# Two PV steps behind fourteen rounds in the MLP's groups of four slots

## The chip, the cores and the metric

The kernel runs on one core of one Trainium2 chip. The metric is the device time of one execution in microseconds, the median of several runs. Its engines are TensorE (PE, with its weight loads shown apart as PEld), VectorE (DVE), ScalarE (ACT), GpSimd (POOL) and SyncE (SP), whose queue issues nearly all DMAs.

## The reference

The program computes `x + s * g` in fp32, for 2048 tokens of width 512. `s` is multi-head attention of the layer-normalised input with 32 heads of width 16, and `g` the SiLU of a two-layer MLP with a squared ReLU.

```python
def _A_ref(x, wqkv, wo):
    B, S, D = x.shape                       # 1, 2048, 512
    H = 32
    Dh = D // H
    qkv = (lambda x, *d: x.transpose(*d))((x @ wqkv).reshape(B, S, 3, H, Dh), 2, 0, 3, 1, 4)
    q, k, v = qkv[0], qkv[1], qkv[2]
    scores = jnp.einsum("bhqd,bhkd->bhqk", q, k) * (Dh ** -0.5)
    p = _softmax(scores, axis=-1)
    o = jnp.einsum("bhqk,bhkd->bhqd", p, v)
    return (lambda x, *d: x.transpose(*d))(o, 0, 2, 1, 3).reshape(B, S, D) @ wo

def _B_ref(x, w1, b1, w2, b2):
    h = jnp.einsum("bsd,df->bsf", x, w1) + b1      # df: 512 x 1792
    zero = jnp.zeros_like(h)
    r = jnp.where(h > zero, h, zero)
    h = r * r
    out = jnp.einsum("bsf,fd->bsd", h, w2) + b2
    return out

x = A_x
xn = _layernorm(x, axis=-1)
s = _A_ref(xn, A_wqkv, A_wo)
g = _silu(_B_ref(xn, B_w1, B_b1, B_w2, B_b2))
return x + s * g
```

## The kernel before

**Two passes over the scores.** The softmax needs the maximum of each row of scores. The kernel computes the scores twice. The first time (`max_mm`, L298 and L305) a matmul puts 128 x 512 scores into a PSUM bank and VectorE reduces them to 128 maxima. The second time (`exp_mm`, matmul at L1234, exp at L1246) a matmul with the maxima folded in as extra rows puts 512 queries against 128 keys into another bank, and ScalarE takes the exp into an SBUF tile. A PV step (`pv_step`, `pv_mm`, L373) then multiplies the exps of four heads with their values into one accumulating bank `po`.

**Units and slots.** A unit is four heads by 512 queries; there are 32. A unit has 16 slots, one for each block of 128 keys, so there are 512 slots. One slot has four maxima (of slot + 24, `LEAD`), four exps and one PV step (of slot - 2).

**Row tiles.** Scores and dense matmuls contract over 64 rows at most, so TensorE is used as two tiles of 64 rows, "lanes" 0 and 1, that run side by side. A round is one operation on each lane. PV contracts over 128 rows with 32 columns a head: four matmuls side by side, and two passes of them to a step, fp32. In the profile the shapes `64*128` and `128*32` tell the two arrangements apart.

**The dense work.** While attention runs, the generator `dense` hands out the MLP and the output projection in pieces. Each matmul of the reference there is three matmuls, of high and low parts (`terms3`). `first_pair` makes two 256-wide halves of the hidden layer in the bank `pd_t`, `second` makes 128 tokens of the output. Both yield groups of work by `block`: 12 units on lane 0 and 12 on lane 1, for four slots. In `first_pair` a unit is two matmuls of 256 columns, in `second` one of 512. The other forms of slot (`slot`, `plain_slot`) do not change here.

**The groups of four slots.** `long_slots` writes out the order of four slots as two halves, `for h in range(2)`. In half `h` the 12 dense units (`D`) stand on lane `h`; beside them are maxima (`m`) and exps (`s`) of the other lane. Before the change a half has two parts: ten rounds of a maximum or an exp beside a unit, then what ends a slot, with its PV step; then four rounds (two units, each beside a maximum; two exps; an exp and a maximum), and the end of the second slot with its PV step. `post`, behind the last unit of a dense bank, lets ScalarE take that bank away: two Relus (L526) for `first_pair`, a copy (L547) for `second`. `last_use` is the ScalarE instruction after which the other lane may write the dense bank.

**What ends and begins a slot.** `max_end` (loads of K and Q for later units, and at a unit's end VectorE's last maximum, L325), `shift_due` (VectorE turns the maxima into the rows that the exps' matmuls use, L335 to L338; they go through DRAM) and `begin`, which sets the clock `now` and runs what `later` has put off until that slot: DMAs, the reciprocal of the sums (`evac_recip`, L397), the tanh of the gate (`gate`, L553) and others.

**Order and buffers.** The program's order on every engine is that in which the code emits (`manual_schedule`), and each engine's queue runs in order. A matmul that waits for a bank holds all that stands behind it. PSUM's eight banks are split between the pools `pe` (3, exps' scores), `pm` (3, maxima's scores), `pd` (1, dense) and `pv` (1, PV):

```python
pe = ph.enter_context(tc.tile_pool(name="pe", bufs=3, space=PSUM))
pm = ph.enter_context(tc.tile_pool(name="pm", bufs=3, space=PSUM))
pd = ph.enter_context(tc.tile_pool(name="pd", bufs=1, space=PSUM))
pv = ph.enter_context(tc.tile_pool(name="pv", bufs=1, space=PSUM))
```

A pool gives its banks out in turn. The tiles of exps in SBUF are a ring of 17 (`NPT`), of which `exp_mm` takes the oldest that no open slot holds.

Of the kernel before, what the change touches and what calls it, by code (L numbers as in the profile page):

```python
# [19 lines left out]
D = 512  # L20
# [8 lines left out]
LEAD = 24  # L29
# [5 lines left out]
EVAC = (1, 6, 7, 9, 11, 14)  # L35
EVAC_LAST = (1, 3, 4, 5, 7, 9)
GAPS = (18, 19, 20, 22)
EPS = 1e-5


@with_exitstack
def kernel(
# [31 lines left out]
    eps_t = const.tile([P, 1], F32, name="eps_t")  # L74
    nc.vector.memset(eps_t, EPS)
    b1_t = const.tile([P, FO], F32, name="b1_t")
# [22 lines left out]
    with ExitStack() as ph:  # L99
# [42 lines left out]
        def load_k(qd, n):  # L142

            p, j, i = n // 6, n // 3 % 2, n % 3
            if n % 6 == 0:
                kas[qd, p] = ring("ka")
            h = 4 * qd + 2 * p + j
            nc.sync.dma_start(
                kas[qd, p][64 * j + DH * i : 64 * j + DH * (i + 1), :].bitcast(F32),
                k_d[h // 8][i % 2, (h % 8) * DH : (h % 8 + 1) * DH, :],  # L150
            )
# [20 lines left out]
        def load_q_pair(u, name, p, tiles):  # L172
                qd, qc = divmod(u, 4)
                t = ring(name)
                for j in range(2):
                    load_head(
                        t, j, q_d, 4 * qd + 2 * p + j, (0, 0, 1), slice(qc * 512, (qc + 1) * 512)
                    )
                tiles.append(t)

        late = []
        last_use = [None]
# [9 lines left out]
        def run_waiting(all_=False):  # L192
            due = [w for w in waiting if all_ or w[0] <= now[0]]
            waiting[:] = [w for w in waiting if w not in due]
            for _, fn in due:
                fn()
# [92 lines left out]
        def max_mm(g, j, bank=None):  # L289
            u = g // 16  # L290
            qd = u // 4
            if u not in mxs:
                mxs[u] = sp.tile([P, 16, 4], F32, name="mx")
                for i in range(2):
                    togo[u, i] = [(p, qb, kc) for p in range(2) for qb in range(4) for kc in range(4)]
            p, qb, kc = togo[u, j].pop(0)
            ps = pm.tile([P, 512], F32, name="pm_t") if bank is None else bank()
            nc.tensor.matmul(  # L298
                ps,
                qms[u][p][64 * j : 64 * j + 64, qb * P : (qb + 1) * P],  # L300
                kas[qd, p][64 * j : 64 * j + 64, kc * 512 : (kc + 1) * 512],
                start=True, stop=True,
            )
            c = (2 * p + j) * 4 + qb
            return nc.vector.tensor_reduce(  # L305
                mxs[u][:, c, kc : kc + 1], ps, axis=AX.X, op=ALU.max
            )

        def max_end(g):
            u, s = divmod(g, 16)  # L310
            if u >= NU:
                return
            qd, qc = divmod(u, 4)
            if qc == 2 and qd + 1 < NQ and s % 2 == 0:
                load_k(qd + 1, s // 2)
            if qc == 3 and qd + 1 < NQ and s % 2 == 0 and s < 8:
                load_k(qd + 1, 8 + s // 2)
            if s in (7, 8):
                load_q_pair(u, "qe", s - 7, qes.setdefault(u, []))
            if s in (9, 11) and u + 1 < NU:  # L320
                load_q_pair(u + 1, "qm", (s - 9) // 2, qms.setdefault(u + 1, []))
            if s == 15:
                assert not togo[u, 0] and not togo[u, 1]
                m4 = m4s[u % 2]
                nc.vector.tensor_reduce(m4[:, :16], mxs[u], axis=AX.X, op=ALU.max)  # L325
                mxs[u] = m4
                late.append((g + 2, u))

        def shift_due(g):
            if late and late[0][0] <= g:  # L330
                shift(late.pop(0)[1])

        def shift(u):
            tr = sp.tile([P, 32], F32, name="tr", bufs=1)
            nc.vector.transpose(tr, mxs[u])  # L335
            sh = sp.tile([P, 2, 32], F32R, name="sh", bufs=1)
            nc.vector.tensor_scalar(sh[:, 0], tr, -1.0, None, op0=ALU.mult)
            nc.vector.scalar_tensor_tensor(  # L338
                sh[:, 1], tr, -1.0, sh[:, 0].bitcast(F32),
                op0=ALU.mult, op1=ALU.subtract,  # L340
            )

            def keep():
                nc.sync.dma_start(
                    sh_d[u].rearrange("b c i n -> (b c) i n"), sh.bitcast(F32)
                )

            def back():
                for p in range(2):
                    for i in range(2):  # L350
                        shift_rows(u, p, i)

            if in_loop:
                later(1, keep)
                later(2, back)
            else:
                keep()
                back()
# [242 lines left out]
        def right(stk, name, bufs):  # L601
            return stk.enter_context(tc.tile_pool(name=name, bufs=bufs, side="right"))
# [75 lines left out]
        def wo_ask(k):  # L678

            c, tt = divmod(k % 16, 4)  # L680
            t0 = c * 512 + tt * P
            g = wos["f"].tile([P, D], F32, name="g", bufs=6)
            nc.sync.dma_start(g, g_d[t0 : t0 + P, :])
            if k < 16:
                t = wos["oc3"].tile([P, D], F32, name="xr", bufs=3)
                nc.sync.dma_start(t, xf[t0 : t0 + P, :])
            elif c < 2:
                t = wos["f"].tile([P, D], F32, name="s")
                nc.sync.dma_start(t, sp_d[t0 : t0 + P, :])
            else:  # L690
                t = tail[c, tt]
            wos[k] = g, t
# [30 lines left out]
        def wo_last(c):  # L723
            for tt in range(4):
                k = 16 + 4 * c + tt
                wo_ask(k + 2)
                if k in GAPS:
                    yield None, None
# [160 lines left out]
        st = right(ln, "wq_st", 1)  # L889
# [296 lines left out]
        for rnd in range(2 * LEAD):  # L1186
# [32 lines left out]
            if g % 2 and g < 16:  # L1219
                c, i = divmod(g // 2, 2)  # L1220
# [29 lines left out]
        def pv_step(st, pts):  # L1250
            u, kb = divmod(st, 16)
            if kb == 0:
                pos[0] = pv.tile([P, 512], F32, name="po")
            pv_mm(pos[0], u // 4, kb, pts)
            if kb == NT - 1:
                if u < NU - 2:
                    evac(pos[0], u)
                elif u == NU - 2:
                    unit_inner(pos[0])
                else:  # L1260
                    unit_final(pos[0])
# [21 lines left out]
        pts = {}  # L1283
# [58 lines left out]
        def long_slots(st0, units, post):  # L1342


            g0 = st0 + LEAD
            todo = [[(st0 + k, j) for k in range(4) for j in (lane, lane + 2)] for lane in range(2)]
            for kb in range(st0, st0 + 4):
                pts.setdefault(kb, {})

            def s(lane):  # L1350
                kb, j = todo[lane].pop(0)
                return exp_mm(kb, j, pts[kb], False)

            for h in range(2):
                own, other = units[h], 1 - h
                for part, (mine, theirs) in enumerate((("D" * 10, "msmsmsmsms"), ("DDss", "mmsm"))):
                    st = st0 + 2 * h + part
                    if st > st0:
                        begin(st)
                    for i, ops in enumerate(zip(mine, theirs)):  # L1360
                        for lane in (h, other) if part else (other, h):
                            o = ops[0] if lane == h else ops[1]
                            if o == "D":
                                own.pop(0)()
                            elif o == "m":
                                max_mm(g0, lane)
                            else:
                                use = s(lane)
                                if part and lane == h and i == 2:
                                    last_use[0] = use  # L1370
                        if part and h and i == 1 and post is not None:
                            post()
                    max_end(st + LEAD)
                    shift_due(st + 1 + LEAD)
                    pv_step(st - 2, pts.pop(st - 2))
            if post is not None:
                last_use[0] = None
            assert not todo[0] and not todo[1] and not units[0] and not units[1]
# [17 lines left out]
        def begin(st):  # L1396
            now[0] = st
            if st % 64 == 48 and st // 64 + 1 < NQ:
                load_v(st // 64 + 1)
            run_waiting()  # L1400
# [63 lines left out]
```

## Time and profile before

| | |
|---|---|
| time, median of 3 runs | 1638.31 us (1637.2 to 1639.26) |
| span of the profiled execution | 1635.6 us |
| granted TensorE clock | 0.999 |
| TensorE matmul busy | 1620.8 us, 99% |
| weight loads busy | 923.2 us, 56% |
| VectorE busy | 1356.8 us, 83% |
| ScalarE busy | 1189.9 us, 73% |
| GpSimd busy | 523.0 us, 32% |

For the profiled execution the span is given, from its first instruction to its last; the time around it isn't shown apart, and the median of the runs is 2.7 us above that span. Busy time of TensorE counts every stretch in which some matmul runs. Matmuls are pipelined, so the start of one to the start of the next is often shorter than a row's duration, and it is the distance between starts that tells the pace. In a timeline, rows of one kind that follow each other are merged, with their count at the end and the time from the first start to the last end.

### The profile page before, as it was taken

To read this page: it belongs to the slowest core of one execution; us is meant where nothing else is said; L and a number is where in the kernel's file an instruction comes from. 1 tells how busy PE (TensorE), PEld (TensorE's weight loads), DVE (VectorE), ACT (ScalarE), POOL (GpSimd) and SP (SyncE) were. 2 spreads that over 40 slices of the span, in tenths; PEclk is the share of its full clock that TensorE was granted. 3 is DMA by queue.
4 is the path that set the end of the run, shared out by engine and by line. 5 is a ranking of instruction groups with operands and counts; after the bars stand their busy time and mean duration, and the time that the engine had idled before them with its cause. 6 is when DMAs were issued, how large, how long until landed. Compare 5 with 4: busy or idle time off the path is not lost.

```text
span 1635.6 us, 35352 instructions
## 1 busy us (share of the span) xinstructions
PE 1620.8 (99%) x13300; PEld 923.2 (56%) x13300; DVE 1356.8 (83%) x2345; ACT 1189.9 (73%) x2351; POOL 523.0 (32%) x547
## 2 busy tenths in 40 slices
PE   8999999999999999999999999999999999999998
PEld 6777565456546655664466456645654565445543
DVE  6356888888888888888888888888888888887754
ACT  7311777777777777877777777777777777777786
POOL 6446568123112311321133112311321233125421
PEclk9999999999999999999999999999999999999999
DMA  8768655434333333434343334323532353246654
GB/s 299 193 210 276 205 171 145 125 100 124 83 95 100 109 93 81 129 87 112 79 121 89 83 90 141 101 68 88 147 98 61 88 144 81 60 130 195 193 170 155
DMA packets 164418, 209.18 MB, mean 128 GB/s; under 512 B 59928, under 2 KB 78872, under 8 KB 162712
## 3 DMA queue, kind: packets, MB, share of 16 engines
q1 hardware_dynamic: 163960, 206.40, 44.5%
q8 instruction: 105, 1.72, 0.5%
q14 instruction: 65, 0.53, 0.1%
q10 hardware_dynamic: 288, 0.52, 0.1%
HBM read 149.95 MB, written 56.61 MB: 126 GB/s over the span
## 4 chain that ended last, share of the span: by engine, by line
PE 99%; DVE 1%; DMA 0%; issue 0%; ACT 0%; POOL 0%; DVEq 0%; POOLq 0%
PE po L373 31%; PE pd_t L242 18%; PE pm_t L298 18%; PE se L1234 15%; PE pd_t L210 6%; PE pd_t L972 2%; PE po L972 2%; PE se L1019 1%; PE se L972 1%; PE pd_t L1019 1%; PE se L298 1%; PE po L1019 1%; PE pm_t L1234 1%; PE pm_t L1065 0%; PE pm_t L811 0%; DVE mx L305 0%
## 5 line engine op out<-in xcount | busy, mean ns | idle before, releaser
L305 DVE TENSOR_REDUCE mx<-pm_t 128x1 f32<-128x512 f32 x2000 | 1245.1, 684 | 167.8 <-PE pm_t L298 77.3
L1246 ACT ACTIVATE pt<-se 128x512 f32<-128x512 f32 x2002 | 1044.2, 617 | 257.6 <-PE se L1234 214.5
L298 PE MATMUL pm_t<-ka,qm 64*128 64x512 f32 x2000 | 793.7, 420 | 1.5 <-DVE mx L305 1.3
L1234 PE MATMUL se<-qe,ka 64*128 64x512 f32 x2002 | 674.0, 396 | 0.2 <-ACT pt L1246 0.2
L373 PE MATMUL po<-pt,v 128*32 128x512 f32 x4096 | 545.3, 604 | 0.0
L298 PEld LDWEIGHTS pm_t<-ka,qm 64*128 64x128 f32 x2000 | 350.1, 184 | 244.8 <-DVE mx L305 230.7
L242 PEld LDWEIGHTS pd_t<-xc,w1s 64*128 64x128 f32 x2688 | 334.0, 187 | 93.9 <-issue 88.9
L242 PE MATMUL pd_t<-xc,w1s 64*128 64x256 f32 x2688 | 380.2, 288 | 0.0
L1234 PEld LDWEIGHTS se<-qe,ka 64*128 64x128 f32 x2002 | 337.6, 184 | 20.7 <-ACT pt L1246 2.6
L242 PE MATMUL pd_t<-w2t,hT 64*128 64x512 f32 x1080 | 300.6, 410 | 0.0
L242 PEld LDWEIGHTS pd_t<-w2t,hT 64*128 64x128 f32 x1080 | 179.1, 184 | 80.5 <-issue 75.5
L529 POOL TENSOR_TENSOR r<-r 128x512 f32<-128x512 f32 x56 | 58.2, 1040 | 374.9 <-ACT r L526 374.9
L373 PEld LDWEIGHTS po<-pt,v 128*32 128x32 f32 x4096 | 81.0, 108 | 158.8 <-issue 136.4
L548 POOL TENSOR_TENSOR u<-u,b_t 128x512 f32<-128x512 f32 x16 | 20.6, 1287 | 316.3 <-ACT u L547 316.3
L411 POOL TENSOR_TENSOR ot<-ot,hl 128x512 f32<-128x512 f32 x31 | 39.8, 1284 | 204.4 <-DMA hl<-r_d 91.1
L210 PE MATMUL pd_t<-wot,oc 64*128 64x512 f32 x336 | 90.9, 406 | 0.0
L526 ACT ACTIVATE r<-pd_t,b_t 128x256 f32<-128x256 f32 x112 | 46.9, 470 | 57.1 <-PE pd_t L242 57.1
L210 PEld LDWEIGHTS pd_t<-wot,oc 64*128 64x128 f32 x336 | 58.4, 184 | 45.4 <-ACT pt L1246 14.2
L84 POOL TENSOR_TENSOR hT<-r,hT 128x512 fp32r<-128x512 f32 x56 | 72.2, 1290 | 4.7
L210 PE MATMUL pd_t<-w2t,hT 64*128 64x512 f32 x264 | 68.8, 393 | 0.0
L305 DVE TENSOR_REDUCE mx<-se 128x1 f32<-128x512 f32 x48 | 32.9, 685 | 40.0 <-PE pm_t L298 30.0
L210 PEld LDWEIGHTS pd_t<-w2t,hT 64*128 64x128 f32 x264 | 47.0, 184 | 6.0
(129 smaller groups left out, 928.5 us busy)
## 6 DMA issues: line engine op xcount, KB each, us to landing
w1s<-w_d SPq DMA_DIRECT2D x196, 256.0 KB
qm<-q_d SPq DMA_DIRECT2D x384, 32.0 KB
ka<-k_d SPq DMA_DIRECT2D x96, 128.0 KB
qe<-q_d SPq DMA_DIRECT2D x384, 32.0 KB
xn_d<-xT SPq DMA_DIRECT2D x8, 1024.0 KB
k_d<-hl SPq DMA_DIRECT2D x32, 256.0 KB
q_d<-hl SPq DMA_DIRECT2D x32, 256.0 KB
xc<-xn_d SPq DMA_DIRECT2D x16, 512.0 KB
```

The lines of the kernel that those rows point to most:

```text
L84: (lo or nc.gpsimd).tensor_tensor(dst[1], raw, dst[0].bitcast(F32), op=ALU.subtract)
L210: mm = nc.tensor.matmul(out_, lh(r), rh(r), start=first_ and lane == 0, stop=last_ and lane == 1, skip_group_check=True,)
L242: mm = nc.tensor.matmul(out_, lh(r), rh(r), start=first_ and lane == 0, stop=last_ and lane == 1, skip_group_check=True,)
L298: nc.tensor.matmul(ps, qms[u][p][64 * j : 64 * j + 64, qb * P : (qb + 1) * P], kas[qd, p][64 * j : 64 * j + 64, kc * 512 : (kc + 1) * 512] ...
L305: return nc.vector.tensor_reduce(mxs[u][:, c, kc : kc + 1], ps, axis=AX.X, op=ALU.max)
L373: nc.tensor.matmul(po[32 * j : 32 * j + 32, :], vs[qd][:, (4 * kb + j) * VW : (4 * kb + j) * VW + 32], pts[j], start=(kb == 0), stop=(kb = ...
L526: nc.scalar.activation(r[:, i], ps[:, i * CW : (i + 1) * CW], AF.Relu, bias=b1_t[:, fo : fo + 1])
L529: nc.gpsimd.tensor_tensor(r, r, r, op=ALU.mult)
L972: nc.tensor.matmul(out_[:, n0:n1], lh(slice(0, P)), rh(slice(0, P))[:, n0:n1], start=first_, stop=last_,)
L1019: nc.tensor.matmul(out_, lh(slice(0, P)), rh(slice(0, P)), start=first_, stop=last_)
L1234: nc.tensor.matmul(se, kas[qd, j // 2][b : b + 64, kb * P : (kb + 1) * P], qes[u][j // 2][b : b + 64, :], start=True, stop=True,)
L1246: return nc.scalar.activation(pts[j], se, AF.Exp, scale=0.25)
```

## The change

In `long_slots` the two parts of a half become one. The order of what stands beside the 12 dense units is written out in `BESIDE`: six maxima and six exps of the other lane. Round 13 is an exp on each lane, round 14 a maximum on each. Then come, for both slots, `max_end` and `shift_due`, and then both PV steps. `begin` of the second slot runs ahead of the eighth round. In each half the dense operation is now written behind the other lane's in every round; `last_use` is the exp of the own lane, the last exp of the half; and `post` follows it. Over a half the counts stay: 12 units, 8 maxima, 8 exps, 2 PV steps. The other lane now has seven maxima and seven exps in a half and the own lane one each, where they had eight and none, and six and two.

```diff
+BESIDE = "msmssmmssmsm"
...
             for h in range(2):
                 own, other = units[h], 1 - h
-                for part, (mine, theirs) in enumerate((("D" * 10, "msmsmsmsms"), ("DDss", "mmsm"))):
-                    st = st0 + 2 * h + part
-                    if st > st0:
-                        begin(st)
-                    for i, ops in enumerate(zip(mine, theirs)):
-                        for lane in (h, other) if part else (other, h):
-                            o = ops[0] if lane == h else ops[1]
-                            if o == "D":
-                                own.pop(0)()
-                            elif o == "m":
-                                max_mm(g0, lane)
-                            else:
-                                use = s(lane)
-                                if part and lane == h and i == 2:
-                                    last_use[0] = use
-                        if part and h and i == 1 and post is not None:
-                            post()
-                    max_end(st + LEAD)
-                    shift_due(st + 1 + LEAD)
-                    pv_step(st - 2, pts.pop(st - 2))
+                st = st0 + 2 * h
+                if h:
+                    begin(st)
+                for i, o in enumerate(BESIDE):
+                    if i == 7:
+                        begin(st + 1)
+                    if o == "m":
+                        max_mm(g0, other)
+                    else:
+                        s(other)
+                    own.pop(0)()
+                s(other)
+                last_use[0] = s(h)
+                if h and post is not None:
+                    post()
+                for lane in (other, h):
+                    max_mm(g0, lane)
+                for k in (st, st + 1):
+                    max_end(k + LEAD)
+                    shift_due(k + 1 + LEAD)
+                for k in (st, st + 1):
+                    pv_step(k - 2, pts.pop(k - 2))
             if post is not None:
                 last_use[0] = None
```

## The prediction

> **What bounds the kernel now.** I read the page's busy times, its chain and its costliest groups first.
>
> ```profile
> span 1635.6 us, 35352 instructions
> PE 1620.8 (99%) x13300; PEld 923.2 (56%) x13300; DVE 1356.8 (83%) x2345; ACT 1189.9 (73%) x2351; POOL 523.0 (32%) x547
> PE 99%; DVE 1%; DMA 0%; issue 0%; ACT 0%; POOL 0%; DVEq 0%; POOLq 0%
> L305 DVE TENSOR_REDUCE mx<-pm_t 128x1 f32<-128x512 f32 x2000 | 1245.1, 684 | 167.8 <-PE pm_t L298 77.3
> L1246 ACT ACTIVATE pt<-se 128x512 f32<-128x512 f32 x2002 | 1044.2, 617 | 257.6 <-PE se L1234 214.5
> ```
>
> TensorE ends everything: the chain is 99% PE. But VectorE is 83% busy, nearly all of it maxima. So PE can be relieved by only a little before the maxima matter.
>
> Next the timeline of TensorE over one half of a group (a half is two slots, one pass of `for h`). Columns: start, duration, engine, line, names, count.
>
> ```profile
> 703.40 0.50 PE L298 MATMUL pm_t<-ka,qm 64*128 64x512 f32 x1
> 703.74 0.39 PE L1234 MATMUL se<-qe,ka 64*128 64x512 f32 x1
> 703.98 0.39 PE L298 MATMUL pm_t<-ka,qm 64*128 64x512 f32 x1
> ...
> 705.62 0.39 PE L1234 MATMUL se<-qe,ka 64*128 64x512 f32 x1
> 705.98 1.07 PE L373 MATMUL po<-pt,v 128*32 128x512 f32 x8
> 706.98 0.49 PE L298 MATMUL pm_t<-ka,qm 64*128 64x512 f32 x1
> ...
> 707.78 0.39 PE L298 MATMUL pm_t<-ka,qm 64*128 64x512 f32 x1
> 708.10 1.07 PE L373 MATMUL po<-pt,v 128*32 128x512 f32 x8
> 709.10 0.49 PE L298 MATMUL pm_t<-ka,qm 64*128 64x512 f32 x1
> ```
>
> Ten rounds, a PV step, four rounds, a PV step, with no hole in it: PE itself is the bound. A round takes 0.235 us (703.74 to 705.62 is eight of them). The first round after a PV step takes 0.34 (703.40 to 703.74), a PV step 1.00 until the next round, and from the last round to the PV step it is 0.32 (707.78 to 708.10) and not 0.235.
>
> How long the halves are, from the same view: 14 halves of first-layer groups (two 256-wide matmuls to a unit) lie between the first two rows, 6 of the second layer (one 512-wide) between the others.
>
> ```profile
> 657.80 0.49 PE L298 MATMUL pm_t<-ka,qm 64*128 64x512 f32 x1
> 737.61 0.50 PE L298 MATMUL pm_t<-ka,qm 64*128 64x512 f32 x1
> 783.30 0.49 PE L298 MATMUL pm_t<-ka,qm 64*128 64x512 f32 x1
> 817.27 0.49 PE L298 MATMUL pm_t<-ka,qm 64*128 64x512 f32 x1
> ```
>
> That is 5.70 and 5.66 us a half. By the loops there are 56 first-layer and 45 second-layer groups, so 112 and 90 halves, 202 in all.
>
> **The change, part by part.**
>
> *Removed: a switch in and out of the PV steps, per half.* The trace has two PV steps behind each other once, at the very end (PE rows, then weight loads of the same stretch):
>
> ```profile
> 1620.07 3.03 PE L373 MATMUL po<-pt,v 128*32 128x512 f32 x24
> ```
>
> ```profile
> 1620.07 0.16 PEld L373 LDWEIGHTS po<-pt,v 128*32 128x32 f32 x8 [0.36 <-issue]
> 1620.53 0.13 PEld L373 LDWEIGHTS po<-pt,v 128*32 128x32 f32 x4 [0.30 <-issue]
> 1620.96 0.13 PEld L373 LDWEIGHTS po<-pt,v 128*32 128x32 f32 x4 [0.30 <-issue]
> 1621.39 0.81 PEld L373 LDWEIGHTS po<-pt,v 128*32 128x32 f32 x8 [0.30 <-ACT pt L1246]
> ```
>
> A step is two sets of four matmuls, and the sets start 0.43 us apart. So a second step adds 0.86, and a pair takes 1.00 + 0.86 = 1.86 until the next round. If nothing waits, the new half is 0.34 + 12 x 0.235 + 0.32 + 1.86 = 5.34 us: 0.36 less, or 0.32 in the second layer. Over 112 and 90 halves that is a gain of about 69 us. The counts of matmuls, maxima and exps are unchanged (per half 8 maxima, 8 exps, 12 units, 2 PV steps).
>
> *Added: waits for score banks.* The maxima's banks (`pm`) are a ring of three, so the matmul of a maximum waits until the reduce of the third one before it has ended. The reduces of the same half, then those of the next half and its exps:
>
> ```profile
> 703.94 3.08 DVE L305 TENSOR_REDUCE mx<-pm_t 128x1 f32<-128x512 f32 x5 [0.20 <-PE pd_t L242]
> 707.55 1.89 DVE L305 TENSOR_REDUCE mx<-pm_t 128x1 f32<-128x512 f32 x3 [0.53 <-PE pd_t L242]
> 709.62 3.08 DVE L305 TENSOR_REDUCE mx<-pm_t 128x1 f32<-128x512 f32 x5 [0.19 <-PE pm_t L298]
> ```
>
> ```profile
> 709.91 2.56 ACT L1246 ACTIVATE pt<-se 128x512 f32<-128x512 f32 x5 [0.36 <-PE pd_t L242]
> 713.52 0.84 ACT L526 ACTIVATE r<-pd_t,b_t 128x256 f32<-128x256 f32 x2 [1.05 <-PE pd_t L242]
> ```
>
> The first reduce starts 0.54 us into the half, and five run without a gap to 3.62 (703.94 + 3.08 - 703.40); one follows the other at about 0.60. In the new half the maxima stand in rounds 1, 3, 6, 7, 10, 12 and two in round 14. The first five are issued by 2.2 us, so their reduces again end at 3.62. The eighth uses the fifth's bank. PE would issue it at 0.34 + 12 x 0.235 = 3.16, but it must wait until 3.62, and the PV pair is queued behind it. Before, the eighth came at 4.38 (707.78) and waited for nothing.
>
> What such a wait looks like where a disturbance already causes it (reduces, then PE, with the maxima at the reduces' pace), and what one costs PE (everything together):
>
> ```profile
> 1379.98 4.87 DVE L305 TENSOR_REDUCE mx<-pm_t 128x1 f32<-128x512 f32 x8
> ```
>
> ```profile
> 1381.31 0.50 PE L298 MATMUL pm_t<-ka,qm 64*128 64x512 f32 x1
> 1381.91 0.49 PE L298 MATMUL pm_t<-ka,qm 64*128 64x512 f32 x1
> 1382.51 0.50 PE L298 MATMUL pm_t<-ka,qm 64*128 64x512 f32 x1
> ```
>
> ```profile
> 637.04 0.18 PEld L298 LDWEIGHTS pm_t<-ka,qm 64*128 64x128 f32 x1 [0.19 <-DVE mx L305]
> 637.11 0.43 PE L298 MATMUL pm_t<-ka,qm 64*128 64x512 f32 x1
> ```
>
> The reduces at 1379.98 end 0.60 apart (4.87 = 0.68 + 7 x 0.60): the second at 1381.26 and the third at 1381.86, and the matmuls come 0.05 later. What waits is the weight load, so the stalled matmul ends 0.50 after it (637.04 to 637.54), and the PV step starts 0.07 before the last matmul's end (707.78 + 0.39 against 708.10).
>
> So the new half: 3.62 + 0.05 + 0.50 - 0.07 = 4.10 for the start of the PV pair, and 4.10 + 1.86 = **5.96 us**. That is 0.26 more than 5.70 and 0.30 more than 5.66: 112 x 0.26 + 90 x 0.30 = 56 us lost, where 69 were to be won.
>
> The exps, also a ring of three banks, come to nearly the same point: five end 3.37 into a half (709.91 + 2.56 - 709.10), the eighth may load at 3.42 and holds its row tile for 0.34; the last maximum's matmul starts behind it on that tile at 3.76, and 0.32 later, 4.08, PV could start. So either wait alone suffices, and freeing one of them alone gives back nearly nothing.
>
> *Moved: `begin` of the second slot, now in the middle of twelve rounds.* Two operations of the delayed list then stand in front of the fifth reduce or the fourth exp:
>
> ```profile
> L397 DVE RECIPROCAL sm<-sm 128x16 f32<-128x16 f32 x31 | 7.5, 243 | 0.4 <-DMA sm<-ot 0.4
> L553 ACT ACTIVATE r<-u 128x512 f32<-128x512 f32 x16 | 10.5, 654 | 0.0
> ```
>
> By their due times 22 reciprocals fall there. Each delays the next reduce by 0.16 (0.243 less the 0.08 by which reduces overlap, 0.68 against 0.60): 3.5 us. Seven tanhs push the exps by about 0.5 (exps follow at 0.48 to 0.50) just where they tie: 3.5 us. Bounds: 0 and 8 together.
>
> *Costed at nothing.* The two Relus now queue behind the eighth exp: that one starts about 4.17 (0.81 + 7 x 0.48), the Relus run from 4.65 to 5.49 (0.84), and the next group's first dense matmul, which needs that bank, comes at 5.96; were the cover gone, 56 groups would pay. The maxima's end and the shift (four VectorE operations of some 0.2 us) now come after the eighth reduce, which ends about 5.40; the next reduce starts at 5.96 + 0.54, so 1.1 us of idle time hides them. `max_end`'s loads for two slots are issued together on SP, up to ten rounds (2.4 us) later, and the shift with its way through DRAM one slot later. Its unit's exps still come five slots behind (some 14 us), and no PE wait for a DMA is in the chain. The weight-part loads stay at units 3, 6, 9 and 12. A late landing would cost at most its own lateness once a unit. The tile ring of exps holds 17: 8 live plus 8 new leave one.
>
> **Sum.** 56 + 7 = +63 us. The profiled execution spans 1635.6, and its time with what lies around it is not given apart; the median of runs is 2.7 above the span. I put the sum on the median: 1638.3 + 63 = **1701 us**. Where the weight load of the waiting matmul hides behind its neighbour (0.1 us a half), 20 less; without the moved operations 7 less: 1674. Where exps start 0.1 later than in the row at 709.91, 20 more: 1721.
>
> **Rivals.**
>
> *The switches go and no bank binds* (the other side): 1638 - 69 = 1569 us. It needs the fifth reduce and the fifth exp done by 3.16; the sign turns where PV starts at 5.70 - 1.86 = 3.84, that is where the fifth reduce ends by 3.36 instead of 3.62 and the exps by 3.13 instead of 3.37. For it: PE is 99% of the chain, and in the trace no bank wait of a normal half is seen. Against it: five reduces in 3.08 us, twice in the rows above.
> The Trainium skill, "TensorEngine Tiling (Array Packing)", Key Properties, says that changing the tiling mode drains TensorE, so by that rule each removed switch is a gain and this rival would be the forecast; the 0.32 against 0.235 and the 1.00 against 0.86 agree with the drain. The same page, under PSUM Bottleneck, warns that tiling speeds up TensorE but not the evacuation of PSUM; as a throughput (8 reduces x 0.60 = 4.8 us) that would still allow 5.34, and only the place of the fifth reduce makes it 5.96.
>
> *The exps bind clearly later than the maxima*: if the exps lie 0.2 us further back than worked out (behind Relus or copies of the half before), PV starts 0.2 later and 202 x 0.2 = 40 is added: 1741. For it: the tie at 4.08 has no slack. Against it: ScalarE has nothing left when a half begins (Relus done at 5.49).
>
> *The gain and the waits cancel*: the last maximum waits only 0.2 us or so, by a hidden weight load and earlier exps: within 3 us of 1638. It would need two of the row-based terms to be off by 0.1 to 0.15 at once, in the same direction.
>
> **How the numbers follow.** Forecast (1674 to 1721) 0.74; exps later 0.11; cancel 0.05, of which 0.03 within 0.2%; the other side 0.08, and 0.02 beyond all of these. 0.2% (3 us) is about what a measurement of this kernel can tell from no change. The range reaches a little over the forecast's bounds, 1668 to 1728, which holds some 0.8. Faster 0.08, same 0.03, slower 0.89.
>
> **What would show it.** After the change: PE rows with 16 PV matmuls in one row of about 1.9 us; the half about 5.96 from first maximum to first maximum; a hole of some 0.5 us on PE ahead of the eighth maximum, whose weight load is put down to VectorE or ScalarE; reduces in runs of eight with about 1.1 us idle between runs, <- PE. The chain should give several per cent to DVE or ACT. Wrong: a half of about 5.34 with no hole; a wait at the head of a half, ahead of the first dense matmul; or PE waiting for a DMA.

## The result and the profile after

The changed kernel takes 1698.5 us (1697.67 to 1699.9) where the kernel before takes 1638.65: a ratio of 1.037, with a 95% interval of 1.0355 to 1.0385. The forecast was 1701. The profiled execution spans 1697.4 us against 1635.6, at a granted clock of 1.000 (0.999 before).

The page of the changed kernel, the rows that answer to those shown of before: busy times, the chain by engine, and the groups of maxima, exps and the weight loads of both (line numbers are one higher than before):

```profile
PE 1679.7 (99%) x13300; PEld 986.7 (58%) x13300; DVE 1342.8 (79%) x2345; ACT 1179.8 (70%) x2351; POOL 523.3 (31%) x547
PE 95%; ACT 3%; DVE 1%; issue 0%; DMA 0%; SPq 0%; DVEq 0%; ACTq 0%
L306 DVE TENSOR_REDUCE mx<-pm_t 128x1 f32<-128x512 f32 x2000 | 1227.8, 682 | 241.7 <-PE pm_t L299 191.0
L1247 ACT ACTIVATE pt<-se 128x512 f32<-128x512 f32 x2002 | 1030.5, 628 | 358.3 <-PE pd_t L243 216.8
L299 PEld LDWEIGHTS pm_t<-ka,qm 64*128 64x128 f32 x2000 | 364.9, 184 | 247.2 <-DVE mx L306 180.5
L1235 PEld LDWEIGHTS se<-qe,ka 64*128 64x128 f32 x2002 | 366.9, 184 | 132.0 <-ACT pt L1247 122.5
```

The weight loads of both before:

```profile
L298 PEld LDWEIGHTS pm_t<-ka,qm 64*128 64x128 f32 x2000 | 350.1, 184 | 244.8 <-DVE mx L305 230.7
L1234 PEld LDWEIGHTS se<-qe,ka 64*128 64x128 f32 x2002 | 337.6, 184 | 20.7 <-ACT pt L1246 2.6
```

The counts of PE, DVE and ACT are the same as before. The chain now runs through ACT and DVE for 4%, before for 1%, and the exps' weight loads wait 122.5 us for ScalarE, where it was 2.6. The maxima's row would mislead: VectorE stands there with 180.5 us and stood there with 230.7 before, when no maximum was late in an ordinary half. Much of that is the 0.84 us in which no weights are loaded at the end of PV (last row of the weight loads below). PE still reads 99% busy, which says little. In the half below the last two exps' matmuls start 0.41 us apart (731.61, and 732.02 by the weight load), and the first one's row fills that whole time, so the wait counts as busy time.

One first-layer half of the changed kernel, from the timeline of TensorE (dense rows and some rounds left out):

```profile
728.59 0.49 PE L299 MATMUL pm_t<-ka,qm 64*128 64x512 f32 x1
728.93 0.39 PE L1235 MATMUL se<-qe,ka 64*128 64x512 f32 x1
...
730.55 0.49 PE L1235 MATMUL se<-qe,ka 64*128 64x512 f32 x1
730.89 0.39 PE L299 MATMUL pm_t<-ka,qm 64*128 64x512 f32 x1
...
731.61 0.91 PE L1235 MATMUL se<-qe,ka 64*128 64x512 f32 x2
732.03 0.73 PE L299 MATMUL pm_t<-ka,qm 64*128 64x512 f32 x2
732.69 1.92 PE L374 MATMUL po<-pt,v 128*32 128x512 f32 x16
734.54 0.50 PE L299 MATMUL pm_t<-ka,qm 64*128 64x512 f32 x1
```

The half takes 5.95 us (728.59 to 734.54), the PV pair begins 4.10 into it, and from its start to the next round it is 1.85. Rounds 13 and 14, which at the paces of before would take 0.56 us (0.24 + 0.32), take 1.08 (731.61 to 732.69). Three more views show why. The reduces run in one piece of eight, with 1.07 and 1.08 us of idle time at its ends; so do the exps, behind the Relus of the half before; and the eighth exp's weight load stands behind ScalarE:

```profile
729.12 4.88 DVE L306 TENSOR_REDUCE mx<-pm_t 128x1 f32<-128x512 f32 x8 [1.07 <-PE pm_t L299]
735.08 1.29 DVE L306 TENSOR_REDUCE mx<-pm_t 128x1 f32<-128x512 f32 x2 [1.08 <-PE pm_t L299]
```

```profile
727.24 0.91 ACT L527 ACTIVATE r<-pd_t,b_t 128x256 f32<-128x256 f32 x2
729.41 4.03 ACT L1247 ACTIVATE pt<-se 128x512 f32<-128x512 f32 x8 [1.27 <-PE pd_t L243]
```

```profile
732.02 0.18 PEld L1235 LDWEIGHTS se<-qe,ka 64*128 64x128 f32 x1 [0.31 <-ACT pt L1247]
732.03 0.41 PEld L299 LDWEIGHTS pm_t<-ka,qm 64*128 64x128 f32 x2
732.69 0.16 PEld L374 LDWEIGHTS po<-pt,v 128*32 128x32 f32 x8 [0.25 <-issue]
734.54 0.18 PEld L299 LDWEIGHTS pm_t<-ka,qm 64*128 64x128 f32 x1 [0.84 <-DVE mx L306]
```

The eighth exp may load at 3.43 (732.02), and the two maxima behind it at 3.44 and, by the end of that merged row, 3.66, which is 0.05 behind the end of the fifth reduce. It is so nearly everywhere: in 194 of the 202 halves the last maximum's weight load begins 0.05 us after the fifth reduce has ended, and in all 202 the last exp's begins 0.05 after the fifth exp. Added over the halves, measured from PV step to PV step, the groups of four slots went from 1149.4 to 1209.4 us: 59.9 of the 61.8 us between the two spans lie in them.

### The profile page after: what moved, and what is told of

It reads as the page before. It is cut to its first block, busy times and chain, and to the rows that moved or that the text cites. A ratio compares the mean times of both kernels' runs of the same rounds, so it can differ in the third digit from the quotient of the medians.

```text
span 1697.4 us, 35499 instructions
## 1 busy us (share of the span) xinstructions
PE 1679.7 (99%) x13300; PEld 986.7 (58%) x13300; DVE 1342.8 (79%) x2345; ACT 1179.8 (70%) x2351; POOL 523.3 (31%) x547
## 4 chain that ended last, share of the span: by engine, by line
PE 95%; ACT 3%; DVE 1%; issue 0%; DMA 0%; SPq 0%; DVEq 0%; ACTq 0%
PE po L374 27%; PE se L1235 20%; PE pm_t L299 18%; PE pd_t L243 14%; PE pd_t L211 5%; ACT pt L1247 3%; PE pd_t L973 2%; PE po L973 2%; PE se L1020 1%; PE se L973 1%; PE pd_t L1020 1%; DVE mx L306 1%; PE se L299 1%; PE po L1020 1%; PE pm_t L1066 0%
## 5 line engine op out<-in xcount | busy, mean ns | idle before, releaser
L306 DVE TENSOR_REDUCE mx<-pm_t 128x1 f32<-128x512 f32 x2000 | 1227.8, 682 | 241.7 <-PE pm_t L299 191.0
L1247 ACT ACTIVATE pt<-se 128x512 f32<-128x512 f32 x2002 | 1030.5, 628 | 358.3 <-PE pd_t L243 216.8
L1235 PE MATMUL se<-qe,ka 64*128 64x512 f32 x2002 | 767.1, 420 | 2.2 <-ACT pt L1247 2.1
L299 PE MATMUL pm_t<-ka,qm 64*128 64x512 f32 x2000 | 766.9, 422 | 2.3 <-DVE mx L306 2.0
L299 PEld LDWEIGHTS pm_t<-ka,qm 64*128 64x128 f32 x2000 | 364.9, 184 | 247.2 <-DVE mx L306 180.5
L374 PE MATMUL po<-pt,v 128*32 128x512 f32 x4096 | 503.5, 600 | 0.0
L1235 PEld LDWEIGHTS se<-qe,ka 64*128 64x128 f32 x2002 | 366.9, 184 | 132.0 <-ACT pt L1247 122.5
L243 PE MATMUL pd_t<-xc,w1s 64*128 64x256 f32 x2688 | 354.1, 285 | 0.0
L243 PE MATMUL pd_t<-w2t,hT 64*128 64x512 f32 x1080 | 285.0, 408 | 0.0
L374 PEld LDWEIGHTS po<-pt,v 128*32 128x32 f32 x4096 | 101.7, 109 | 209.4 <-issue 200.8
L211 PE MATMUL pd_t<-w2t,hT 64*128 64x512 f32 x264 | 68.5, 392 | 0.0
```

What stands on the lines that cost most here:

```text
L211: mm = nc.tensor.matmul(out_, lh(r), rh(r), start=first_ and lane == 0, stop=last_ and lane == 1, skip_group_check=True,)
L243: mm = nc.tensor.matmul(out_, lh(r), rh(r), start=first_ and lane == 0, stop=last_ and lane == 1, skip_group_check=True,)
L299: nc.tensor.matmul(ps, qms[u][p][64 * j : 64 * j + 64, qb * P : (qb + 1) * P], kas[qd, p][64 * j : 64 * j + 64, kc * 512 : (kc + 1) * 512] ...
L306: return nc.vector.tensor_reduce(mxs[u][:, c, kc : kc + 1], ps, axis=AX.X, op=ALU.max)
L374: nc.tensor.matmul(po[32 * j : 32 * j + 32, :], vs[qd][:, (4 * kb + j) * VW : (4 * kb + j) * VW + 32], pts[j], start=(kb == 0), stop=(kb = ...
L1235: nc.tensor.matmul(se, kas[qd, j // 2][b : b + 64, kb * P : (kb + 1) * P], qes[u][j // 2][b : b + 64, :], start=True, stop=True,)
```

## The experiments

### Is it the banks, and which?

Four runs shorten what empties the banks, in the changed order and in the old one. They leave out part of the work: a reduce looks at half of its scores, an exp does half of its queries, and the other half of each tile of exps holds ones. Short maxima have the first of these edits, short exps the other two:

```diff
-mxs[u][:, c, kc : kc + 1], ps, axis=AX.X, op=ALU.max
+mxs[u][:, c, kc : kc + 1], ps[:, :256], axis=AX.X, op=ALU.max
...
+                for t in rot["pt"]:
+                    nc.gpsimd.memset(t[:, 256:], 1.0)
...
-return nc.scalar.activation(pts[j], se, AF.Exp, scale=0.25)
+return nc.scalar.activation(pts[j][:, :256], se[:, :256], AF.Exp, scale=0.25)
```

Short maxima, changed order:

> The changed kernel, with each reduce over 256 of its 512 columns (the shift is then a maximum over half of the scores, so it is part of the work left out). Theory (both rings of three banks hold the half back, at 4.10 by the reduces and 4.08 by the exps): the exps still hold PV at 4.08, so nearly nothing comes back, 1690 to 1697 us; the half stays at 5.93 or so. Rival 1 (the maxima alone bind): the half falls to 5.34 and the time to about 1572. Rival 2 (no bank binds, TensorE is slower in the new order): 1698.

Measured: 1687.4 us (1686.89 to 1688.57), 2.6 below the range expected. Short exps, changed order:

> The changed kernel, with each exp over 256 of its 512 queries (the other half of each tile of exps stays at 1, so half of the exps are left out). Theory: the reduces still hold the eighth maximum to 3.62, the half stays at 5.95, and only the seven tanhs stop costing (7 x 0.5): 1692 to 1697 us. Rival 1 (the exps alone bind): 1572. Rival 2 (no bank binds): 1698.

Measured: 1692.3 us (1690.26 to 1694.38). Both short, changed order:

> The changed kernel, with both the reduces and the exps over 256 columns. Theory: no bank is late, the half is 5.34 in the first layer and 5.31 in the second, and the time falls by 112 x 0.61 + 90 x 0.64 = 126 us and the 6 us of reciprocals and tanhs, to about 1567; TensorE has no hole ahead of the PV pair. Rival 2 (no bank binds, the new order is slow on TensorE itself): about 1698.

Measured: 1572.7 us (1571.87 to 1573.6), where about 1567 was expected. Both short, old order:

> The kernel before, with the reduces and the exps over 256 columns as in the run beside it. Theory: TensorE alone bounds the groups of four slots there, so nothing is won in them: 1630 to 1639 us, the half at 5.70 and 5.66; the pair of PV steps, freed of its waits, is then worth about 69 us against this one. Rival (the kernel before too waits for banks, so that shorter operations would speed up any order): clearly under 1600.

Measured: 1628.6 us (1627.59 to 1628.86), 1.4 below the range expected.

Either ring alone gives back 11 us (maxima) or 6 (exps); both together give back 126. So both hold the half at nearly the same point, as the prediction worked out: with short maxima the last exp's weight load still begins 0.05 us after the fifth exp in all 202 halves, with short exps the last maximum's 0.05 after the fifth reduce in all 202. By the traces 8, 3 and 119 of the 11, 6 and 126 us lie in the groups' halves; the rest is won in other slots. With short exps the seven halves with a tanh are back at 5.95, but six second-layer halves of 6.1 to 6.5 us stand in the trace (three with full exps), and their cause stays open. In the old order the same shortening is worth 10 us, but only 2 of them in the halves (1149.4 to 1147.2), so there TensorE did bound them. With short operations the pair of PV steps is worth 1628.6 - 1572.7 = 56 us (69 by the prediction).

With short maxima the exps alone pace the end of the half. Weight loads of TensorE there:

```profile
665.53 0.18 PEld L1235 LDWEIGHTS se<-qe,ka 64*128 64x128 f32 x1 [0.28 <-ACT pt L1247]
666.02 0.18 PEld L1235 LDWEIGHTS se<-qe,ka 64*128 64x128 f32 x1 [0.19 <-ACT pt L1247]
666.51 0.18 PEld L1235 LDWEIGHTS se<-qe,ka 64*128 64x128 f32 x1 [0.19 <-ACT pt L1247]
667.00 0.18 PEld L1235 LDWEIGHTS se<-qe,ka 64*128 64x128 f32 x1 [0.30 <-ACT pt L1247]
```

The last four exps' matmuls follow each other at 0.49 us, close to the exps' own 0.48 (4.03 us for eight, above), and wait for a bank each time. With both short there is no such row in the half below (first layer, with two dense units shown):

```profile
663.43 0.49 PE L299 MATMUL pm_t<-ka,qm 64*128 64x512 f32 x1
663.77 0.39 PE L1237 MATMUL se<-qe,ka 64*128 64x512 f32 x1
663.78 0.40 PE L243 MATMUL pd_t<-xc,w1s 64*128 64x256 f32 x2
...
666.08 0.39 PE L299 MATMUL pm_t<-ka,qm 64*128 64x512 f32 x1
666.17 0.40 PE L243 MATMUL pd_t<-xc,w1s 64*128 64x256 f32 x2
...
666.53 0.50 PE L299 MATMUL pm_t<-ka,qm 64*128 64x512 f32 x2
666.96 1.92 PE L374 MATMUL po<-pt,v 128*32 128x512 f32 x16
668.82 0.50 PE L299 MATMUL pm_t<-ka,qm 64*128 64x512 f32 x1
```

This half takes 5.39 us, and the PV pair starts at 3.53. In the second layer's halves, 5.37 long, the banks are not quite out of the way. In one of them (from 301.23 us) the fifth reduce ends at 304.25, and the last maximum's weights are loaded at 304.31. That maximum's matmul comes 0.31 us behind the one before it on its lane, where 0.23 is the pace (medians of 0.33 and 0.23 over the 90 halves).

### Is it the pair, or the order?

The pair alone: in the old order the first PV step is moved behind the 14 rounds. `begin`, `max_end` and the exps and maxima stay.

```diff
                     shift_due(st + 1 + LEAD)
-                    pv_step(st - 2, pts.pop(st - 2))
+                    if part:
+                        for k in (st - 1, st):
+                            pv_step(k - 2, pts.pop(k - 2))
```

> The kernel before with one thing moved: the first PV step of each half stands behind the 14 rounds, next to the second. The old order of exps and maxima, begin, max_end and shift_due stay. Theory (the pair of PV steps takes away the time in which VectorE and ScalarE free banks; the order is nearly indifferent): the fifth reduce still ends at 3.62 and the eighth maximum, now due at about 3.16, waits for it, so the half is again 5.95; the reciprocals and tanhs stand behind the fifth reduce and exp and cost nothing: 1690 to 1696 us. Rival (the new order of exps and maxima is what costs, the pair is a gain): about 1569 to 1600.

Measured: 1690.2 us (1689.78 to 1690.43), against 1637.4 for the kernel before on the same chip, a ratio of 1.0319 (1.0304 to 1.0335). TensorE's rows at the end of a half, and the reduces:

```profile
726.24 0.50 PE L298 MATMUL pm_t<-ka,qm 64*128 64x512 f32 x1
726.83 0.50 PE L298 MATMUL pm_t<-ka,qm 64*128 64x512 f32 x1
...
727.43 0.50 PE L298 MATMUL pm_t<-ka,qm 64*128 64x512 f32 x1
727.86 1.92 PE L373 MATMUL po<-pt,v 128*32 128x512 f32 x16
729.71 0.49 PE L298 MATMUL pm_t<-ka,qm 64*128 64x512 f32 x1
```

```profile
724.29 4.87 DVE L305 TENSOR_REDUCE mx<-pm_t 128x1 f32<-128x512 f32 x8 [1.08 <-PE pd_t L242]
```

Here the last three maxima stand 0.60 apart, the reduces' pace, and the half is again 5.95. So the pair alone costs 53 us, and in its trace the halves with a tanh or a reciprocal are 5.95 like the others, as expected.

What the order alone costs took three runs. The first is the changed kernel with only the first PV step put back behind round ten:

```diff
                     own.pop(0)()
+                    if i == 9:
+                        pv_step(st - 2, pts.pop(st - 2))
...
-                for k in (st, st + 1):
-                    pv_step(k - 2, pts.pop(k - 2))
+                pv_step(st - 1, pts.pop(st - 1))
```

> The changed kernel with the first PV step put back behind the tenth round; the new order of exps and maxima, the place of begin and the joint end of both slots stay. Theory: the eighth maximum comes at 4.4 again, no bank is late, the half is 5.70 and 5.66: 1636 to 1641 us. Rival (the order or the moved begin costs by itself): 1655 to 1698.

Measured: 1705.4 us (1705.05 to 1705.86). This expectation was wrong by some 65 us, and the run is slower than the one with the pair. One place behind a first-layer group (ScalarE's Relus, then TensorE):

```profile
731.50 0.85 ACT L527 ACTIVATE r<-pd_t,b_t 128x256 f32<-128x256 f32 x2
```

```profile
731.65 0.50 PE L299 MATMUL pm_t<-ka,qm 64*128 64x512 f32 x1
732.41 0.38 PE L243 MATMUL pd_t<-xc,w1s 64*128 64x256 f32 x1 [0.26 <-ACT r L527]
```

The Relus end at 732.35, and the next group's first dense matmul, due with the maximum at 731.65, waits for them until 732.41. In the changed kernel the Relus stand behind the last exp too, but the pair hides them: in the view above they end at 728.15, and the next group begins at 728.59. I put `post` back behind the last unit, everything else as in this run:

```diff
-                s(other)
-                last_use[0] = s(h)
                 if h and post is not None:
                     post()
+                s(other)
+                last_use[0] = s(h)
```

> The run with the new order and the first PV step behind round ten, with one thing put back: post (the Relus or the copy that take the dense bank away) stands behind the last unit, ahead of the last two exps. Theory: the miss of that run is mostly post behind the last exp, which a pair of PV steps (1.86 us) hides and a single one (1.00) does not. Its trace has the halves behind a first-layer group at 6.45 where the others are 5.74 (56 of them), and those behind a second-layer group's copy at 6.24 (7 of them): 56 x 0.71 + 7 x 0.50 = 43 us come back, 1657 to 1666 us. Rival (the order of exps and maxima, or the moved begin, is what costs): above 1690.

Measured: 1662.15 us (1661.7 to 1663.36): the 43 us, with 24 us still left over the kernel before. Then everything but the order went back to its old place (PV step, `max_end`, `shift_due` and `begin` together behind round ten, `post` behind the last unit):

```diff
-                    if i == 7:
+                    if i == 10:
+                        max_end(st + LEAD)
+                        shift_due(st + 1 + LEAD)
+                        pv_step(st - 2, pts.pop(st - 2))
                         begin(st + 1)
...
-                s(other)
-                last_use[0] = s(h)
                 if h and post is not None:
                     post()
+                s(other)
+                last_use[0] = s(h)
...
-                for k in (st, st + 1):
-                    max_end(k + LEAD)
-                    shift_due(k + 1 + LEAD)
-                for k in (st, st + 1):
-                    pv_step(k - 2, pts.pop(k - 2))
+                max_end(st + 1 + LEAD)
+                shift_due(st + 2 + LEAD)
+                pv_step(st - 1, pts.pop(st - 1))
```

> The new order of exps and maxima alone: the first PV step, the end of the first slot and begin of the second stand together behind round ten as before, and post behind the last unit. Theory: nothing is late but the last exp of a half, which the next half's first dense matmul waits for and which comes about 0.03 later than before (5.74 against 5.70 in the run with the split): 1638 + 202 x 0.03, so 1638 to 1647 us. Rival (the order costs by itself, by waits for banks): 1655 or more.

Measured: 1649.2 us (1648.92 to 1649.6), a ratio of 1.007 (1.0053 to 1.0087) to 1637.8 for the kernel before beside it. It lies 2 us above the range expected. The wait that was expected, at the head of a half, is there, but there is a second one in the ninth round. TensorE's matmuls over two first-layer halves, then a weight load of the second one:

```profile
839.48 0.49 PE L299 MATMUL pm_t<-ka,qm 64*128 64x512 f32 x1
839.50 0.50 PE L243 MATMUL pd_t<-xc,w1s 64*128 64x256 f32 x2
...
845.21 0.50 PE L299 MATMUL pm_t<-ka,qm 64*128 64x512 f32 x1
845.21 0.50 PE L243 MATMUL pd_t<-xc,w1s 64*128 64x256 f32 x2
...
847.18 0.50 PE L1235 MATMUL se<-qe,ka 64*128 64x512 f32 x1
847.23 0.46 PE L243 MATMUL pd_t<-xc,w1s 64*128 64x256 f32 x2
847.51 0.39 PE L299 MATMUL pm_t<-ka,qm 64*128 64x512 f32 x1
847.53 0.40 PE L243 MATMUL pd_t<-xc,w1s 64*128 64x256 f32 x2
```

```profile
847.17 0.18 PEld L1235 LDWEIGHTS se<-qe,ka 64*128 64x128 f32 x1
```

In the first of the two the dense lane starts 0.03 us late (839.50 for 839.48), behind the exp that it has to wait for, as expected, and keeps its pace of 0.24 us a unit up to the PV step. In the second one it starts on time. But the order puts exps in rounds 8 and 9 next to each other. The second of them is the fifth, needs the second one's bank (that exp ends at 847.13), and loads late, which holds the dense unit beside it too: 0.30 us to the next one for 0.24. The first layer's halves divide evenly between the two kinds, with medians of 5.74 and 5.76 for 5.70 before; in the second layer most halves have both waits (5.74 for 5.66). No run has one of the two waits alone. The late fifth exp is also at 730.55 in the changed kernel (0.34 to the next round), where the later wait swallows it. The 13 us between this run and the one before it belong to the joint end of both slots and to `begin` with a single PV step behind them; what of either, was not separated.

### The moved begin

```diff
                 if h:
                     begin(st)
+                begin(st + 1)
                 for i, o in enumerate(BESIDE):
-                    if i == 7:
-                        begin(st + 1)
```

> The changed kernel with begin of the second slot at the head of the half, in place of the middle of its rounds. Theory: 22 reciprocals and 7 tanhs then fall into the idle time of VectorE and ScalarE at the head of a half; the trace of the changed kernel shows 0.10 and 0.51 us more in such halves, so 22 x 0.10 + 7 x 0.51 = 6 us come back: about 1692.5. Rival (the longer halves have another cause): 1698.

Measured: 1694.9 us (1694.47 to 1696.28), 3.6 us less than the changed kernel, where 6 were expected. The halves with a reciprocal are 5.95 again, but those with a tanh still take 6.36 (6.46 in the changed kernel). ScalarE there:

```profile
676.83 0.69 ACT L548 ACTIVATE u<-pd_t 128x512 f32<-128x512 f32 x1
678.90 0.63 ACT L554 ACTIVATE r<-u 128x512 f32<-128x512 f32 x1 [1.39 <-POOL u L549]
```

The tanh needs GpSimd's addition of the bias, which comes behind the copy at 676.83, so ScalarE is idle for 1.39 us until it can start. The half begins at 678.17, and the tanh ends 1.36 us into it, where the first exp of the half shown of the changed kernel starts at 0.82 (729.41). So the exps behind the tanh are late all the same.

## Why the prediction was right

**The sum.** The new half was to be 5.96 with PV at 4.10; it is 5.95 with PV at 4.10. By the trace the wait in every half adds 202 x 5.95 - 1149.4 = 53 us (56 in the prediction), and the pair alone, run by itself, costs 53. The moved operations add some 6 (7 in the prediction). Together that is 59 of the 60 us by which the run is slower.

**The step that decided it** was that the eighth maximum waits for the fifth reduce. The run with the pair alone shows it in the maxima's distance of 0.60. With both operations short it nearly goes, and the pair gains 56 us over the old order with the same operations. That the exps hold the half at nearly the same point, so that freeing one ring gives back nearly nothing, held as well: 11 and 6 us of the 126 that both give.

**The gain that was lost** was sized 69 us and measures 56 with short operations. The term that was off is the undisturbed half of 5.34: there it is 5.39 in the first layer and 5.37 in the second. In the first layer the step that failed is the round of 0.235 us. That was the distance of the exps' and maxima's starts; a dense unit of two 256-wide matmuls takes 0.24 (ten of them take 2.39, from 663.78 to 666.17, and the other lane's ten rounds 2.31), so after twelve rounds the dense lane is behind. In the second layer the last maximum still waits for its bank. So 56 us is not the price of the switches alone, but what the pair is worth in these two runs. None of it had a part in the forecast, because the waits end later.

**The moved operations** were put at 7 us. The seven tanhs cost 0.51 each as said (halves of 6.45 to 6.47, and none left of them with short exps). The 22 reciprocals cost 0.10 and not 0.16 each. VectorE's rows of such a half give the distances:

```profile
711.17 2.48 DVE L306 TENSOR_REDUCE mx<-pm_t 128x1 f32<-128x512 f32 x4 [1.07 <-PE pm_t L299]
713.57 0.24 DVE L398 RECIPROCAL sm<-sm 128x16 f32<-128x16 f32 x1
713.73 2.42 DVE L306 TENSOR_REDUCE mx<-pm_t 128x1 f32<-128x512 f32 x4
```

The next reduce does start 0.16 after the reciprocal's start. But it ends sooner: four reduces take 2.48 us ahead of the reciprocal and 2.42 behind it. So the eighth one ends at 716.15, 4.98 after the first one's start, where it is 4.88 without a reciprocal, and the half grows by the same 0.10 (5.95 to 6.05). With short exps these halves are 6.05 as well, so the exps have no part in it.

**Costed at nothing** were the Relus behind the last exp. The cover named was the pair; the run with the split shows the price without it, 56 halves of 0.71. The loads and the shift moved later did not show: no wait of TensorE for a DMA stands in the changed kernel's chain (DMA 0%).

**The rivals.** That the switches go and the banks hardly bind is what happens with short operations, 1572.7 us. That number is near the 1569 worked out for the full ones by chance, as the short operations also win a little in other slots. That the exps bind clearly later did not happen: the last exp's weights are loaded 3.43 us into the half, 3.42 by the prediction. That gain and waits cancel would have needed a shorter wait than the one measured. The Trainium skill, "TensorEngine Tiling (Array Packing)", Key Properties, says that changing the tiling mode drains TensorE. The trace agrees so far as a change costs time: with short operations the halves differ by 57.5 us (1147.2 to 1089.7), 0.28 us for each switch in and out that is saved. No run parts a drain from other costs of such a switch. The warning of the Trainium skill, "TensorEngine Tiling (Array Packing)", PSUM Bottleneck, that tiling speeds up TensorE but not the evacuation of PSUM, is the one that decides here, though not as a throughput: VectorE is busy 79% of the time and idle for 1.1 us in each half.

## What to carry to other kernels

Before joining two pieces of work that need no fresh bank, count what the engines that empty the banks do meanwhile. Here, when the fifth reduce ends, VectorE has three left, 3 x 0.60 us. The next one can only come 0.49 us (to PV), 1.85 (the pair) and 0.53 (the next half up to its first reduce) later, and the 1.07 us between are lost in every half. A rule that can be read off a timeline of this kernel: the last matmul ahead of the piece cannot start before the operation that empties the bank three back has ended, and all behind it in the queue waits too. Where two rings end at the same point, test both together, since either alone gave back 6 to 11 us here and both 126. Whether deeper rings would do it was not run; all eight banks are in use.

## What the runs showed of the hardware

A PV step by itself takes 1.00 us to the next round and a second one behind it adds 0.85, and that holds over a whole kernel: the pair takes 1.85 in all 202 halves of each run that has it. A matmul that waits for a bank shows in its weight load, which begins 0.05 us after the bank's operation has ended; TensorE's busy share stays at 99%. A reciprocal of 0.24 us between two reduces starts the next one 0.16 later and ends it 0.10 later. And one wait may hide another in the same place: the new order of exps and maxima costs 11 us with the PV steps apart and nothing beside the pair, where the halves are 5.95 in the old order and in the new.
